# A fused attention and FFN kernel: FFN blocks of 384 tokens with 128-wide f tiles, operands placed at multiples of 512 bytes, and x split at the turn of blocks

## The chip, the cores and the metric

The kernel runs on one core of one Trainium2 chip. The metric is the device time of one execution in microseconds (us). Three executions of the kernel before took 975.67, 976.66 and 978.05 us, a median of 976.66 us.

## What is computed

The inputs q, k and v have 8 batches, 8 heads, 576 positions and a head size of 64. The output of the attention, reshaped to 4608 tokens of 512 values, is the x of a feed-forward layer (FFN) with 2048 hidden values.

```python
q_d, k_d, v_d = mean of q, k, v over groups of 4 positions        # 144 positions
out_up = np.repeat(softmax_attention(q_d, k_d, v_d), 4, axis=2)
mask = np.abs(pos[:, None] - pos[None, :]) < 4                    # 7 neighbours
out_local = softmax(where(mask, 0.125 * q @ k.T, -1e9)) @ v
x = (out_up + out_local).transpose(0, 2, 1, 3).reshape(4608, 512)
h = x @ w_in                                                      # 512 -> 2048
g = s * maximum(h, 0) ** 2 + b
out = g @ w_out                                                   # 2048 -> 512
```

## The kernel before

**The FFN.** Every float32 operand of the FFN is split into a high part in the type float32r and a low part, and each product is made of three matmuls (high by high, high by low, low by high). The tokens go in 18 blocks of 256 (`TB`), and the 2048 hidden values in 8 tiles of 256, numbered p. One step is one block t and one tile p. `gemm1(t, p)` makes 24 matmuls of 256 columns (lines 544 to 546): two halves j of the f tile, four k tiles, three products each. The stationary operand is a 128x128 piece of `wi`, the moving one is 256 tokens of `xh` or `xl`. ScalarE then makes relu, square and the high part `gh` (lines 554 to 556), VectorE the low part `gl` (line 557); every third of these pairs from block 3 on is one tile `gb` instead. `gemm2(t, p)` (lines 589 to 591) makes 12 matmuls of 512 columns: two groups m of 128 tokens, two halves j, three products. Here `gh` or `gl` is stationary and `wo` is moving, and the sum stays in PSUM over all eight p, one bank for each m. In all there are 3456 matmuls of 256 columns and 1728 of 512. After the last p VectorE scales the sums and adds the bias into `os` (lines 596 and 601), and SyncE's queue stores it.

**The split of x.** `split_x(t)` makes `xh` on ScalarE (line 530, one copy of 128x1024, two where a block crosses a batch) and `xl` on VectorE (line 531). From block 3 on it is called three steps before the block begins (`splits`), into tiles with two buffers, so a block's x stands ready while the one before it is still multiplied.

**The attention.** The 12 pairs of heads of the first three batches are done by `first_unit`, whose local part runs on TensorE; the other 20 pairs, two at a time, by `two_pairs`, whose local part runs on GpSimd (`pr`, line 455; part of `acc`, line 477) and VectorE (`st`, line 457; `pv`, line 476), seven neighbours at a time. `advance` hands out pieces of the attention between the steps of the FFN so that a batch is complete a few steps before its tokens are needed (`need`, `free`).

**The order.** The instructions of each engine are put in order at build time from the order in the code and priorities (`tc.high_priority`), and run in that order, each waiting on semaphores. For steps from block 3 on, `gemm2` follows its `gemm1` by three steps (`pend`).

**Where the tiles lie.** Pools hand out SBUF addresses at build time. Start addresses modulo 512 bytes in each partition, read from the two built programs:

| tile | before | after |
|---|---|---|
| wi, wo of p = 2 to 6 | 352 | 0 |
| wi, wo of p = 0, 1, 7 | 480 | 0 |
| xh, xl, gh, gl | 288 | 0 |
| xh, xl of block 2; gb; os | 352 | 0 |

Every 128-column slice of these tiles is 512 bytes long, so the slices that a matmul reads have the remainder of their tile. Before, all these remainders are 32 modulo 64.

Of the kernel before, what the change touches and what calls it, by code (L numbers as in the profile page):

```python
# [10 lines left out]
F32 = mybir.dt.float32  # L11
# [24 lines left out]
TB = 256  # L36
NB = NT // TB
# [14 lines left out]
BEHIND = {1: 400, 2: 100, 4: 100, 5: 400}  # L52
HF = 7
# [4 lines left out]
OB = {0: (0, 1), 1: (2, 3), 2: (6, 7)}  # L58
# [3 lines left out]
def attention_ffn_kernel(ctx, tc, qk, vw_in, vr_in, vdm, qkn, vn, w_in, w_out, s_in, b_in, out):  # L62
# [24 lines left out]

    def make_room(i):
        sc, dg = flat(f"wi{6 - i}", 2048), flat(f"wo{6 - i}", 2048)
# [41 lines left out]
    mask = cst.tile([P, 3, 32], F32, name="mask")  # L131
# [103 lines left out]
    def split_w(p):  # L235
        with tc.high_priority(offset=-BEHIND.get(p, 0)):
            split_parts(p)
# [95 lines left out]
    def first_unit(b, hp, banks):  # L333
# [75 lines left out]
        ups = tmp([P, SD], "ups")  # L409
# [107 lines left out]
    def split_x(t):  # L517
        tags = ("os", "xl2") if t == 2 else ("xh", "xl")
        pool = one if t == 2 else two
        xh = pool.tile([P, HP, TB], F32R, tag=tags[0], name="xh")  # L520
        xl = pool.tile([P, HP, TB], F32R, tag=tags[1], name="xl")
        t0 = t * TB
        while t0 < (t + 1) * TB:
            b = t0 // S
            while (b, HP - 1) not in complete:
                next(gen)
            n = min((t + 1) * TB, (b + 1) * S) - t0
            src = xt[b][:, :, t0 - b * S : t0 - b * S + n]
            dst = slice(t0 - t * TB, t0 - t * TB + n)
            nc.scalar.copy(xh[:, :, dst], src)  # L530
            nc.vector.tensor_tensor(
                xl[:, :, dst], src, xh[:, :, dst].bitcast(F32), ALU.subtract)
            t0 += n
        xs[t] = (xh, xl)
# [4 lines left out]
    def gemm1(t, p):  # L539
        xh, xl = xs[t]  # L540
        ph = bank(6 if t >= 3 and p % 2 else 7 if t == 1 and p < HF else 4, [P, 2, TB], "ph")
        for j, k in itertools.product(range(2), range(NK)):
            f = slice(P * j, P * j + P)
            nc.tensor.matmul(ph[:, j], wi[p][:, 0, k, f], xh[:, k], start=(k == 0), stop=False)  # L544
            nc.tensor.matmul(ph[:, j], wi[p][:, 0, k, f], xl[:, k], start=False, stop=False)  # L545
            nc.tensor.matmul(ph[:, j], wi[p][:, 1, k, f], xh[:, k], start=False, stop=(k == NK - 1))  # L546
        if t >= 3 and p % 3 == 2:
            both = one.tile([P, 2, 2, TB], F32R, tag="xl2", name="gb")
            gh, gl = both[:, 0], both[:, 1]
        else:  # L550
            gh = two.tile([P, 2, TB], F32R, tag="gh", name="gh")
            gl = two.tile([P, 2, TB], F32R, tag="gl", name="gl")
# [5 lines left out]
        gt[(t, p)] = (gh, gl)  # L558
# [15 lines left out]
    def gemm2(t, p):  # L574
        if (t, p) == (0, NFP - 1):
            column_sums()
        gh, gl = gt.pop((t, p))
        if p == 0:
            ob = OB.get(t, OB[0])
            oacc[t] = [bank(i, [P, DM], "po") for i in ob]  # L580
        po = oacc[t]
        end = t == NB - 1 and p == NFP - 1
        os_ = one.tile([P, 2, DM], F32, tag="os", name="os") if p == NFP - 1 else None
        for m in range(2):
            ms = slice(P * m, P * m + P)
            for j in range(2):
                first = p == 0 and j == 0
                last = p == NFP - 1 and j == 1
                nc.tensor.matmul(po[m], gh[:, j, ms], wo[p][:, 0, j], start=first, stop=False)  # L589
# [9 lines left out]
        if p == NFP - 1 and not end:  # L599
            for m in range(2):  # L600
                nc.vector.scalar_tensor_tensor(
                    os_[:, m], po[m], sb_s, bias, ALU.mult, ALU.add)
# [155 lines left out]
```

## Time and profile before

| | |
|---|---|
| median of three runs | 976.66 us |
| the profiled execution's own time | 974.94 us |
| its span, first to last instruction | 973.1 us |
| mean granted TensorE clock | 0.982 |
| busy: TensorE | 937.4 us (96%) |
| busy: VectorE | 646.8 us (66%) |
| busy: ScalarE | 478.8 us (49%) |
| busy: GpSimd | 425.0 us (44%) |

The profile is one execution, recorded instruction by instruction. In its rows PE is the matmuls of TensorE, PEld its weight loads, DVE is VectorE, ACT ScalarE, POOL GpSimd and SP SyncE; an engine with a q behind it is its queue. `out<-in` are the names of tiles, and a shape is partitions by elements. A row of the timeline gives the start in us, the duration in us, and the instruction; rows that follow on the same line are merged, with their number behind the x. The recorded end of a matmul is modelled and overlaps its successors (a matmul of 256 columns is given 0.28 us, while the next one starts 0.11 to 0.12 us later). So the distance from start to start, not the duration, tells how fast matmuls flow.

### The profile page before, as it was taken

The page shows a single profiled execution, that of the slowest core. Times are in us where ns is not written, and L with a number is a line of the kernel's source. Part 1 is how long each engine was busy: PE and PEld are TensorE (multiplying, and loading weights), DVE is VectorE, ACT ScalarE, POOL GpSimd, SP SyncE. Part 2 cuts the span into 40 slices and gives each one's busy share as a digit, 9 for nine tenths or more (in the row PEclk, how much of TensorE's full clock was granted, in tenths as well). Part 3 has the DMA queues.
Part 4 walks back from the last instruction along what each step waited for, and adds up shares of the span by engine and source line. Part 5 has one row for each costly group of instructions (what it writes and reads, how often), then busy time and mean ns, then how long its engine had stood idle before and what let it go on. Part 6 is the DMA issues. An engine that isn't in the chain of part 4 may idle for free.

```text
span 973.1 us, 18535 instructions
## 1 busy us (share of the span) xinstructions
PE 937.4 (96%) x7316; PEld 840.0 (86%) x7316; DVE 646.8 (66%) x1175; ACT 478.8 (49%) x1141; POOL 425.0 (44%) x455
## 2 busy tenths in 40 slices
PE   5769999999999999999999999999999999999998
PEld 4558888788999989889989898999899999998997
DVE  5999985864468778878787975876787772211121
ACT  5878775453755454534545344454454444333231
POOL 9422011100167686776767585575776750000000
PEclk9579999999999999999999999999999999999999
DMA  9746422102233232322323232231323100000000
GB/s 314 261 132 204 166 65 73 60 31 86 88 122 112 86 101 85 133 65 72 106 93 102 80 98 80 78 112 58 112 90 111 55 23 1 23 1 22 1 23 22
DMA packets 32103, 86.26 MB, mean 89 GB/s; under 512 B 3344, under 2 KB 7952, under 8 KB 32016
## 3 DMA queue, kind: packets, MB, share of 16 engines
q1 hardware_dynamic: 32016, 85.08, 26.4%
q8 instruction: 57, 0.93, 0.4%
q14 instruction: 30, 0.25, 0.1%
HBM read 75.63 MB, written 9.44 MB: 87 GB/s over the span
## 4 chain that ended last, share of the span: by engine, by line
PE 76%; DVE 7%; POOL 6%; DMA 6%; issue 3%; ACT 2%; DVEq 0%; SPq 0%; POOLq 0%; ACTq 0%
PE ph L544 12%; PE ph L545 12%; PE ph L546 12%; PE po L589 11%; PE po L590 11%; PE po L591 11%; DMA tqk<-in_qk_dram 3%; POOL pr L455 2%; PE sa L297 2%; DMA lqk<-in_qkn_dram 1%; POOL acc L477 1%; DMA wst<-in_moe_w_out_dram 1%; PE up L328 1%; PE ol L420 1%; PE ot L486 1%
## 5 line engine op out<-in xcount | busy, mean ns | idle before, releaser
L544 PE MATMUL ph<-xh,wi 128*128 128x256 f32 x1152 | 327.2, 284 | 5.3 <-DVE gl L557 2.5
L545 PE MATMUL ph<-xl,wi 128*128 128x256 f32 x1152 | 324.0, 281 | 0.0
L546 PE MATMUL ph<-xh,wi 128*128 128x256 f32 x1152 | 323.6, 281 | 0.0
L455 POOL TENSOR_TENSOR pr<-lqk 128x576 f32<-128x576 f32 x140 | 203.0, 1473 | 90.1 <-DMA lqk<-in_qkn_dram 53.9
L544 PEld LDWEIGHTS ph<-xh,wi 128*128 128x128 f32 x1152 | 217.1, 188 | 12.8 <-DVE gl L557 3.4
L545 PEld LDWEIGHTS ph<-xl,wi 128*128 128x128 f32 x1152 | 217.0, 188 | 5.0 <-issue 0.2
L546 PEld LDWEIGHTS ph<-xh,wi 128*128 128x128 f32 x1152 | 217.3, 189 | 0.1
L554 ACT ACTIVATE ph<-ph 128x512 f32<-128x512 f32 x144 | 83.7, 581 | 236.7 <-PE ph L546 236.5
L589 PE MATMUL po<-wo,gh 128*128 128x512 f32 x456 | 183.0, 402 | 0.2 <-ACT gh L556 0.2
L590 PE MATMUL po<-wo,gh 128*128 128x512 f32 x456 | 181.5, 398 | 0.0
L591 PE MATMUL po<-wo,gl 128*128 128x512 f32 x456 | 179.5, 399 | 0.0
L557 DVE TENSOR_TENSOR gl<-ph,gh 128x512 fp32r<-128x512 f32 x114 | 77.9, 683 | 110.9 <-ACT gh L556 110.5
L477 POOL TENSOR_TENSOR acc<-acc,pv 128x576 f32<-128x576 f32 x80 | 114.6, 1433 | 68.0 <-DVE acc L477 33.5
L457 DVE TENSOR_REDUCE st<-pr 128x9 f32<-128x576 f32 x140 | 105.9, 756 | 40.9 <-POOL pr L455 38.8
L287 POOL TENSOR_TENSOR dq<-vq 64x64 f32<-64x64 f32 x58 | 25.6, 441 | 192.4 <-PE up L326 190.2
L556 ACT CAST gh<-ph 128x512 fp32r<-128x512 f32 x114 | 66.8, 586 | 70.6 <-PE po L590 68.5
L591 PEld LDWEIGHTS po<-wo,gl 128*128 128x128 f32 x456 | 85.7, 188 | 17.3 <-issue 0.2
L476 DVE TENSOR_TENSOR pv<-lv,st 128x576 f32<-128x576 f32 x120 | 87.2, 747 | 20.2 <-POOL acc L477 19.6
L589 PEld LDWEIGHTS po<-wo,gh 128*128 128x128 f32 x456 | 85.7, 188 | 15.8 <-ACT gh L556 0.8
L590 PEld LDWEIGHTS po<-wo,gh 128*128 128x128 f32 x456 | 85.8, 188 | 15.6
L555 ACT ACTIVATE ph<-ph 128x512 f32<-128x512 f32 x144 | 83.8, 582 | 3.4
L590 PE MATMUL po<-wo,gb 128*128 128x512 f32 x120 | 48.2, 402 | 0.0
(145 smaller groups left out, 1261.1 us busy)
## 6 DMA issues: line engine op xcount, KB each, us to landing
tqk<-in_qk_dram SPq DMA_DIRECT2D x30, 584.0 KB, 4.0
lqk<-in_qkn_dram SPq DMA_DIRECT2D x20, 768.0 KB, 4.4
lv<-in_vn_dram SPq DMA_DIRECT2D x20, 480.0 KB, 3.5
out_dram<-os SPq DMA_DIRECT2D x17, 512.0 KB, 3.0
wst<-in_moe_w_in_dram SPq DMA_DIRECT2D x7, 1024.0 KB, 5.5
wst<-in_moe_w_out_dram SPq DMA_DIRECT2D x7, 1024.0 KB, 5.3
tvd<-in_vdm_dram SPq DMA_DIRECT2D x29, 160.0 KB, 2.7
tvr<-in_vr_dram SPq DMA_DIRECT2D x29, 128.0 KB, 2.1
```

The source lines that it names most:

```text
L455: nc.gpsimd.tensor_tensor(pr, lqk[:, 0:CH], lqk[:, CH + o : 2 * CH + o], ALU.mult)
L457: nc.vector.tensor_reduce(ls[:, :, o], pr, AX.X, ALU.add)
L476: nc.vector.tensor_tensor(pv, lv[:, o : o + CH], w, ALU.mult)
L477: (nc.vector if o % 3 == 1 else nc.gpsimd).tensor_tensor(acc[:, :, h], acc[:, :, h], pv, ALU.add)
L544: nc.tensor.matmul(ph[:, j], wi[p][:, 0, k, f], xh[:, k], start=(k == 0), stop=False)
L545: nc.tensor.matmul(ph[:, j], wi[p][:, 0, k, f], xl[:, k], start=False, stop=False)
L546: nc.tensor.matmul(ph[:, j], wi[p][:, 1, k, f], xh[:, k], start=False, stop=(k == NK - 1))
L554: nc.scalar.activation(ph, ph, AF.Relu)
L555: nc.scalar.activation(ph, ph, AF.Square)
L589: nc.tensor.matmul(po[m], gh[:, j, ms], wo[p][:, 0, j], start=first, stop=False)
L590: nc.tensor.matmul(po[m], gh[:, j, ms], wo[p][:, 1, j], start=False, stop=False)
L591: nc.tensor.matmul(po[m], gl[:, j, ms], wo[p][:, 0, j], start=False, stop=last)
```

## The change

The first three blocks keep 256 tokens and their steps. From token 768 on there are ten blocks of 384 tokens, 13 blocks in all. A step of these has one 128-wide f tile: `gemm1` makes 12 matmuls of 384 columns, `gemm2` 9 of 512 (three groups m of 128 tokens). There are 16 such steps to a block, 160 in all. Blocks of 384 keep three PSUM banks (0, 1, 2) for the sums, and the attention of the later batches cycles through two banks (3, 5) where it had three. Small unused tiles (`skip`) of 32, 448 and 96 bytes move the FFN's tiles to the remainders in the table above; to make room, the attention's `mask` shares the place of `pv`, and `ups` that of `ptm`. From block 3 on x is split in two halves of two k tiles each, with two buffers for a half, so a half can be written only when the block before has finished with that half: `split_x(n + 1)` is called at the last step of block n (the turn), at high priority, and there two `gemm2` are taken from `pend` instead of one. Each group m of `os` is stored by its own DMA, and the third group uses the place of the first.

```diff
-TB = 256
-NB = NT // TB
+BLOCKS = [(t, 256) for t in range(0, 768, 256)] + [(t, 384) for t in range(768, NT, 384)]
+NB = len(BLOCKS)
...
+AHEAD = 6
+SKIP = (32, 448, 96)
-OB = {0: (0, 1), 1: (2, 3), 2: (6, 7)}
+OB = {0: (0, 1), 1: (2, 3), 2: (6, 7), 3: (0, 1, 2)}
...
+    def skip(n, pool=one):
+        pool.tile([P, n // 4], F32, tag=f"skip{n}", name="skip")
...
-    def split_x(t):
-        tags = ("os", "xl2") if t == 2 else ("xh", "xl")
...
+    def split_x(n):
+        t0, nt = BLOCKS[n]
+        nk = NK if n < 3 else NK // 2
+        hs, ls = [], []
+        for k0 in range(0, NK, nk):
+            tags = ("os", "xl2") if n == 2 else ("xh", "xl")
+            pool = one if n == 2 else two
+            xh = pool.tile([P, nk, nt], F32R, tag=tags[0], name="xh")
+            xl = pool.tile([P, nk, nt], F32R, tag=tags[1], name="xl")
...
+                src = xt[b][:, k0 : k0 + nk, at - b * S : at - b * S + m]
+                nc.scalar.copy(xh[:, :, dst], src)
+                nc.vector.tensor_tensor(
+                    xl[:, :, dst], src, xh[:, :, dst].bitcast(F32), ALU.subtract)
...
+    def tiles(n, i):
+        return (i, (0, 1)) if n < 3 else (i // 2, (i % 2,))
+
+    def gemm1(n, i, st):
+        p, js = tiles(n, i)
+        shape = [P, len(js), BLOCKS[n][1]]
...
-        for m in range(2):
+        for m in range(nt // P):
...
+                nc.vector.scalar_tensor_tensor(
+                    os_[:, m % 2, cs], po[m][:, cs], sb_s, bias[:, cs], ALU.mult, ALU.add)
+                nc.sync.dma_start(out[r0 : r0 + P, cs], os_[:, m % 2, cs])
...
-    need = [0, 2 * HF - 3] + [(S * b // TB) * NFP - 3 for b in range(2, B)]
-    free = [0, 0, 16] + [((S * (b - 1) - 1) // TB) * NFP - 2 for b in range(3, B)]
-    rings = {1: banks(5, 6), 2: banks(5), 3: banks(2, 3, 5)}
+    need = [0, 2 * HF - 3] + [begin(S * b) - (10 if b == 2 else AHEAD) for b in range(2, B)]
+    free = [0, 0, 16] + [max(need[b - 1], begin(S * (b - 1) - 1) - AHEAD) for b in range(3, B)]
+    rings = {1: banks(5, 6), 2: banks(5), 3: banks(3, 5)}
...
-    splits = {(1, HF - 1): 2, (2, NFP - 2): 3}
-    splits.update({(t, NFP - 3): t + 1 for t in range(3, NB - 1)})
+    splits = {(1, HF - 1): 2}
...
+        turn = 2 <= n < NB - 1 and i == (NFP if n < 3 else 2 * NFP) - 1
+        if turn:
+            with tc.high_priority():
+                split_x(n + 1)
-        if len(pend) > (2 if t < 3 else 3):
+        while len(pend) > (2 if n < 3 or turn else 3):
             gemm2(*pend.pop(0))
```

The changed file is longer, so its line numbers are higher: lines 544 to 546 of `gemm1` become 571 to 573, lines 554 to 557 become 581 to 584, lines 589 to 591 of `gemm2` become 618 to 620, lines 530 and 531 of `split_x` become 549 and 550, and line 601 becomes 629.

How the order changes is shown at three places. First TensorE, where the last block begins; the numbers behind names tell one buffer's use from another's. Before, the first matmul of the block (`ph_10502`) follows the second product group of a `gemm2`:

```order
L589 MATMUL po_10314<-wo_1446,gh_10352 128x512
L590 MATMUL po_10314<-wo_1446,gh_10352 128x512
L591 MATMUL po_10314<-wo_1446,gl_10353 128x512
L544 MATMUL ph_10502<-xh_10412,wi_705 128x256 [waits DVE_49]
L545 MATMUL ph_10502<-xl_10413,wi_705 128x256
L546 MATMUL ph_10502<-xh_10412,wi_705 128x256
```

And now, with the two halves of x in `xh_9721`, `xl_9722` and `xh_9725`, `xl_9726`:

```order
L619 MATMUL po_9388<-wo_1994,gh_9688 128x512
L571 MATMUL ph_9747<-xh_9721,wi_707 128x384 [waits DVE_49,PE_49]
L572 MATMUL ph_9747<-xl_9722,wi_707 128x384
...
L571 MATMUL ph_9747<-xh_9725,wi_707 128x384 [waits Activation_49]
L620 MATMUL po_9386<-wo_1994,gl_9689 128x512
L620 MATMUL po_9387<-wo_1994,gl_9689 128x512
L620 MATMUL po_9388<-wo_1994,gl_9689 128x512
L618 MATMUL po_9386<-wo_1994,gb_9716 128x512 [waits Activation_49]
L619 MATMUL po_9386<-wo_1994,gb_9716 128x512
L572 MATMUL ph_9747<-xl_9726,wi_707 128x384 [waits DVE_49]
```

The block's first step is now cut in three by waits on ScalarE and VectorE, with five matmuls of earlier `gemm2` between; the 18 matmuls of `gemm2` ahead of it are not all shown.

Second VectorE, where x is split while GpSimd and VectorE work on the attention. Before, one subtract of 1024 columns stands between the sums of the attention (`st`):

```order
L457 TENSOR_REDUCE st_6585<-pr_6605 128x9 [waits DVE_49]
L531 TENSOR_TENSOR xl_6891<-x_4704,xh_6890 128x1024 [waits PE_49,Activation_49]
L457 TENSOR_REDUCE st_6585<-pr_6608 128x9 [waits DVE_49,Pool_49]
L557 TENSOR_TENSOR gl_6457<-ph_6431,gh_6456 128x512 [waits PE_49,Activation_49]
L457 TENSOR_REDUCE st_6585<-pr_6655 128x9 [waits DVE_49,Pool_49]
```

And now, at the turn that begins the block of `xh_6187`:

```order
L487 TENSOR_TENSOR acc_5865<-lv_6078,st_5866 128x9x64 [waits DMAHW3_49,DVE_49]
L490 TENSOR_TENSOR pv_6213<-lv_6078,st_5866 128x576
L490 TENSOR_TENSOR pv_6216<-lv_6078,st_5866 128x576
L550 TENSOR_TENSOR xl_6188<-x_4490,xh_6187 128x768 [waits Activation_49]
L320 RECIPROCAL dsm_6109<-dsm_6109 96x3 [waits Activation_49]
L491 TENSOR_TENSOR acc_5865<-acc_5865,pv_6213 128x9x64 [waits DVE_49]
L285 TENSOR_REDUCE qd_6528<-tqk_6325 128x144 [waits DMAHW7_49]
L550 TENSOR_TENSOR xl_6192<-x_4490,xh_6191 128x768 [waits PE_49,Activation_49]
L584 TENSOR_TENSOR gl_6159<-ph_6145,gh_6158 128x384 [waits PE_49,Activation_49]
```

The two halves stand behind work of the attention, one of them behind an instruction that waits for a DMA.

Third VectorE again, where a block's sums leave PSUM near the end. Before, both groups leave one behind the other:

```order
L557 TENSOR_TENSOR gl_10176<-ph_10150,gh_10175 128x512 [waits DVE_49,PE_49,Activation_49]
L601 SCALAR_TENSOR_TENSOR os_10266<-po_9961,sb_s_168,bias_143 128x512 [waits DMAHW2_49,PE_49]
L601 SCALAR_TENSOR_TENSOR os_10266<-po_9962,sb_s_168,bias_143 128x512 [waits PE_49]
L557 TENSOR_TENSOR gl_10219<-ph_10193,gh_10218 128x512 [waits DVE_49,Activation_49]
L557 TENSOR_TENSOR gb_10261<-ph_10236,gb_10261 128x512 [waits PE_49,Activation_49]
```

And now:

```order
L584 TENSOR_TENSOR gl_9761<-ph_9747,gh_9760 128x384 [waits DVE_49,PE_49,Activation_49]
L629 SCALAR_TENSOR_TENSOR os_9812<-po_9386,sb_s_169,bias_144 128x512 [waits DMAHW1_49,DMAHW0_49,PE_49]
L629 SCALAR_TENSOR_TENSOR os_9812<-po_9387,sb_s_169,bias_144 128x512 [waits PE_49]
L584 TENSOR_TENSOR gl_9780<-ph_9766,gh_9779 128x384 [waits DVE_49,Activation_49]
L629 SCALAR_TENSOR_TENSOR os_9812<-po_9388,sb_s_169,bias_144 128x512 [waits DMAHW2_49,DVE_49,PE_49]
```

The third group's instruction has a wait for a DMA, the store of the first group.

More of the change, by code (lines that the diff above doesn't have):

```diff
@@ L536, in attention_ffn_kernel @@
     gt = {}
     oacc = {}
[L539 to L548, printed above, removed]
+    def tiles(n, i):
+        return (i, (0, 1)) if n < 3 else (i // 2, (i % 2,))
@@ new lines, in gemm1 @@
+    def gemm1(n, i, st):
+        xh, xl = xs[n]
+        p, js = tiles(n, i)
+        shape = [P, len(js), BLOCKS[n][1]]
+        ph = bank(6 if n >= 3 and i % 2 else 7 if n == 1 and p < HF else 4, shape, "ph")
+        for j, k in itertools.product(js, range(NK)):
+            o, f = ph[:, js.index(j)], slice(P * j, P * j + P)
+            nc.tensor.matmul(o, wi[p][:, 0, k, f], xh[k], start=(k == 0), stop=False)
+            nc.tensor.matmul(o, wi[p][:, 0, k, f], xl[k], start=False, stop=False)
+            nc.tensor.matmul(o, wi[p][:, 1, k, f], xh[k], start=False, stop=(k == NK - 1))
+        if n >= 3 and st % 3 == 2:
+            both = one.tile([P, 2, *shape[1:]], F32R, tag="xl2", name="gb")
@@ L572, in column_sums, with gemm2 @@
         nc.vector.tensor_scalar(bias, cs, sb_b, None, ALU.mult)
-    def gemm2(t, p):
-        if (t, p) == (0, NFP - 1):
+    def gemm2(n, i):
+        if (n, i) == (0, NFP - 1):
             column_sums()
[L577 to L583, printed above, removed]
-        for m in range(2):
-            ms = slice(P * m, P * m + P)
[L586 to L589, printed above, removed]
-                nc.tensor.matmul(po[m], gh[:, j, ms], wo[p][:, 1, j], start=False, stop=False)
-                nc.tensor.matmul(po[m], gl[:, j, ms], wo[p][:, 0, j], start=False, stop=last)
-            if end:
-                r0 = TB * t + P * m
-                for c in (0, DM // 2):
-                    cs = slice(c, c + DM // 2)
-                    nc.vector.scalar_tensor_tensor(
-                        os_[:, m, cs], po[m][:, cs], sb_s, bias[:, cs], ALU.mult, ALU.add)
-                    nc.sync.dma_start(out[r0 : r0 + P, cs], os_[:, m, cs])
-        if p == NFP - 1 and not end:
-            for m in range(2):
@@ new lines, in gemm2 @@
+        gh, gl = gt.pop((n, i))
+        p, js = tiles(n, i)
+        t0, nt = BLOCKS[n]
+        if i == 0:
+            oacc[n] = [bank(j, [P, DM], "po") for j in OB[min(n, 3)]]
+        po = oacc[n]
+        done = p == NFP - 1 and js[-1] == 1
+        end = done and n == NB - 1
+        if done:
+            os_ = one.tile([P, 2, DM], F32, tag="os", name="os")
+        for m in range(nt // P):
+            ms = slice(P * m, P * m + P)
+            for c, j in enumerate(js):
+                first, last = i == 0 and c == 0, done and j == 1
+                nc.tensor.matmul(po[m], gh[:, c, ms], wo[p][:, 0, j], start=first, stop=False)
+                nc.tensor.matmul(po[m], gh[:, c, ms], wo[p][:, 1, j], start=False, stop=False)
+                nc.tensor.matmul(po[m], gl[:, c, ms], wo[p][:, 0, j], start=False, stop=last)
+            if not done:
+                continue
+            if end and m == 2:
+                os_ = one.tile([P, 2, DM], F32, tag="big", name="os")
+            r0 = t0 + P * m
+            w = DM // 2 if end and m == 2 else DM
+            for c in range(0, DM, w):
+                cs = slice(c, c + w)
```

59 lines of the change are left out of this document (29 added, 30 removed).

## The prediction

> **What bounds the kernel now.** I read the busy table and the slices first:
>
> ```profile
> PE 937.4 (96%) x7316; PEld 840.0 (86%) x7316; DVE 646.8 (66%) x1175; ACT 478.8 (49%) x1141; POOL 425.0 (44%) x455
> ...
> PEclk9579999999999999999999999999999999999999
> ```
>
> TensorE is busy almost throughout and its clock is full after the first slices. The windows by stage say the same:
>
> ```profile
> 40.00:100.00 60.00, 47.61 (x525) 42.06 (x526) 59.19 (x119) 47.96 (x105) 13.09 (x14) 0.83 0.50 168
> 100.00:300.00 200.00, 197.87 (x1898) 173.74 (x1898) 140.11 (x269) 115.50 (x280) 39.45 (x54) 1.00 0.24 80
> 300.00:760.00 460.00, 457.23 (x3051) 414.88 (x3050) 356.03 (x618) 216.25 (x534) 316.29 (x293) 1.00 0.29 93
> 760.00:969.00 209.00, 209.00 (x1352) 188.99 (x1351) 62.43 (x108) 73.38 (x144) 25.78 (x23) 1.00 0.05 17
> ```
>
> From 100 us on TensorE is idle for about 1% of a window or less. VectorE, in third place, is busy 77% of the stretch from 300 to 760 us, GpSimd, in fifth, 69%. The waits of TensorE hold almost nothing that belongs to the FFN:
>
> ```profile
> PE ph L544 <- DVE gl L557: 2.5, 3, 1.2
> ```
>
> So the time is set by how fast the FFN's matmuls follow each other, and that is read from start to start. TensorE's rows late in the program, where the attention is over, at places that I name below:
>
> ```profile
> 938.76 0.28 PE L544 MATMUL ph<-xh,wi 128*128 128x256 f32 x1
> ...
> 939.46 0.28 PE L544 MATMUL ph<-xh,wi 128*128 128x256 f32 x1
> ...
> 941.50 0.39 PE L589 MATMUL po<-wo,gh 128*128 128x512 f32 x1
> ...
> 948.42 0.39 PE L589 MATMUL po<-wo,gb 128*128 128x512 f32 x1
> ...
> 949.78 0.28 PE L544 MATMUL ph<-xh,wi 128*128 128x256 f32 x1
> ...
> 952.61 0.40 PE L589 MATMUL po<-wo,gh 128*128 128x512 f32 x1
> ```
>
> A step of `gemm1`, 24 matmuls, takes 2.74 us from 938.76 to 941.50 (0.1142 each; its last 18, from 939.46, 0.1133) and 2.83 us from 949.78 to 952.61 (0.1179), though nothing is waited for and the shapes are the same. Six of `gemm2` take 1.36 us from 948.42 to 949.78 (0.2267 each). The last 48 matmuls of the program are all of `gemm2`:
>
> ```profile
> 958.21 0.39 PE L589 MATMUL po<-wo,gh 128*128 128x512 f32 x1
> ...
> 966.45 0.40 PE L589 MATMUL po<-wo,gh 128*128 128x512 f32 x1
> ...
> 967.85 0.40 PE L589 MATMUL po<-wo,gh 128*128 128x512 f32 x1
> ```
>
> ```profile
> 969.02 0.39 PE L591 MATMUL po<-wo,gl 128*128 128x512 f32 x1
> ```
>
> From the first to the last, 47 distances, it is 10.81 us, 0.2300 each, and the six from 966.45 take 0.2333 each. Block 2, whose x lies elsewhere, gives a third pace for 256 columns:
>
> ```profile
> 200.67 0.28 PE L545 MATMUL ph<-xl,wi 128*128 128x256 f32 x1
> ...
> 203.43 0.39 PE L591 MATMUL po<-wo,gl 128*128 128x512 f32 x1
> ```
>
> That is 23 distances in 2.76 us, 0.1200 each. With 0.116 for 256 columns (between the two late steps) and 0.230 for 512, the FFN takes 3456 x 0.116 + 1728 x 0.230 = 798 us of the span of 973.1.
>
> **The change part by part. The pace.** The same shapes go at 0.1133, 0.1179 and 0.1200, and at 0.2267 and 0.2333. The extremes lie 6.7 and 6.6 ns apart, so the loss seems to come in pieces of 6.7 ns. What differs between these steps is where the operands lie and how the matmuls came in from the step before. If the best rows hold one such piece in 256 columns and two in 512, then 0.1067 and 0.2133 are left without loss, both 0.417 ns a column. That is an estimate, but another row supports it. The attention's plain float32 transposes run slowly enough per column not to be pressed:
>
> ```profile
> 377.40 1.20 PE L486 MATMUL ot<-ident,acc 128*128 128x128 f32 x9
> 378.35 0.36 PE L544 MATMUL ph<-xh,wi 128*128 128x256 f32 x1
> ```
>
> Nine of 128 columns take 0.95 us, 0.825 ns a column. Half of that is 0.4125, if float32r goes at twice the pace of plain float32. No row shows float32r matmuls with operands at multiples of 512 bytes, so the ends are these. Low: 0.4125 ns a column, 0.1056, 0.1584 and 0.2112 for 256, 384 and 512. High: 0.1200, its 1.5 times 0.1800, and 0.2333. After the change there are 24 steps with 24 matmuls of 256 (576), 160 steps with 12 of 384 (1920), and still 1728 of 512. The low end is 60.8 + 304.1 + 364.9 = 730 us, a gain of 68; the high end is 69.1 + 345.6 + 403.1 = 818, a loss of 20. I take 0.422 ns a column, 0.108, 0.162 and 0.216, which is nearer to the transposes' row than to the best float32r row (0.443): the loss changes with placement, and now every slice begins on a 512-byte line and ends on one. That makes 62.2 + 311.0 + 373.2 = 746 us, **a gain of 52**. Fewer and longer matmuls are in this count; by columns alone `gemm1` has as many as before.
>
> The page TensorE: Matmul & The Clock Gate of the Trainium skill, section Back-to-back issue gap, gives N/2.4 + 2.5 ns as the isolated gap from matmul to matmul on the warm clock. By it the FFN would take 62.9 + 312.0 + 372.9 = 748 us; the rows above lie 4 to 10% over it, and it says nothing of addresses.
>
> **The turn.** Ten times x is now split with TensorE at the end of a block, where it was done three steps ahead. Each half costs a copy on ScalarE and a subtract on VectorE:
>
> ```profile
> L531 DVE TENSOR_TENSOR xl<-x,xh 128x1024 fp32r<-128x1024 f32 x12 | 26.3, 2188 | 12.5 <-ACT xh L530 12.4
> ...
> L531 DVE TENSOR_TENSOR xl<-x,xh 128x512 fp32r<-128x512 f32 x4 | 2.7, 686 | 1.8 <-ACT xh L530 1.8
> ...
> L530 ACT CAST xh<-x 128x768 fp32r<-128x768 f32 x4 | 3.3, 829 | 1.0 <-DVE x L423 0.6 <-DVE x L490 0.4
> ```
>
> The first half is free after six of the last step's twelve matmuls. A copy of 0.83 and a subtract of about 1.03 (1.5 times 0.686) make it ready 1.9 us later; the second half is free 1.0 us later and, behind a relu, ready 3.3 us after the first was freed. TensorE has six matmuls of `gemm1` and 18 of `gemm2` to do first, 0.97 + 3.89 = 4.9 us. Without other work on VectorE the turn costs nothing. But while GpSimd works the subtract is stretched:
>
> ```profile
> 532.55 5.79 DVE L531 TENSOR_TENSOR xl<-x,xh 128x1024 fp32r<-128x1024 f32 x1
> ```
>
> The mean of 1024 columns above is 2.19 us, this one took 5.79. At that rate a half takes 4.3 us, and instructions of the attention stand ahead of it. Token 4032, the first of the last batch, lies in block 11, so the attention ends six steps before that block, and eight of the ten turns have it beside them. At worst each is late by about 4 us, at best by nothing: 0 to 32 us. I take 1 us each, **a cost of 8**, nearer the low end since TensorE also has five matmuls of `gemm2` to put between.
>
> **The shorter step and the stores.** A step falls from 24 x 0.116 + 12 x 0.230 = 5.5 us to 12 x 0.162 + 9 x 0.216 = 3.9. A bank of `ph` is used again two steps later, so relu, square, copy and `gl` must be through in about 5.8 us where they had 8.3.
>
> ```profile
> L554 ACT ACTIVATE ph<-ph 128x512 f32<-128x512 f32 x144 | 83.7, 581 | 236.7 <-PE ph L546 236.5
> ...
> L557 DVE TENSOR_TENSOR gl<-ph,gh 128x512 fp32r<-128x512 f32 x114 | 77.9, 683 | 110.9 <-ACT gh L556 110.5
> ...
> L556 ACT CAST gh<-ph 128x512 fp32r<-128x512 f32 x114 | 66.8, 586 | 70.6 <-PE po L590 68.5 <-PE po L591 1.0
> ...
> L601 DVE SCALAR_TENSOR_TENSOR os<-po,sb_s,bias 128x512 f32<-128x512 f32 x34 | 24.8, 743 | 7.0 <-PE po L591 4.6 <-DMA out_dram<-os 2.4
> ```
>
> The relu, a square like it, the copy and `gl` take 0.58 + 0.58 + 0.59 + 0.68 = 2.4 us at 512 columns and less at 384, so they fit unless VectorE's queue holds several us of attention. The same attention in a stretch that is 6% shorter makes VectorE 82% and GpSimd 74% busy there. The third group of a block's sums waits for the store of the first:
>
> ```profile
> out_dram<-os SPq DMA_DIRECT2D x17, 512.0 KB, 3.0
> ```
>
> A store lands 3.0 us after its issue, and the third sum is done 1.3 us after the first, so VectorE can stand for some 2 us nine times; queued behind it are `gl` of the next steps, and TensorE waits for these only after its 5.8 us are gone. I put this at nothing; with that cover gone it would be 18. For the whole paragraph I take **a cost of 6**, between 0 and 20. The two-bank ring of the attention and the moved tiles `mask` and `ups` I put at nothing: the matmuls that they could delay stand between FFN matmuls that hide them.
>
> **The sum** for the profiled execution is 974.9 - 52 + 8 + 6 = 937 us. The median of the runs lies 1.7 above that execution, so I predict **939 us**, with a range of its own from 920 to 955 (a gain of 68 and a cost of 12, a gain of 45 and a cost of 24).
>
> **The rivals.** (1) Only the best pace of today is reached everywhere: 0.1133, 0.170 and 0.2267. Then the FFN is 65.3 + 326.4 + 391.7 = 783, a gain of 15 against a cost of 14: 976 us. For it speaks that all rows of float32r lie at or over 0.443 ns a column, against it that the loss comes in pieces that change with the steps. (2) The pace is reached, but from 300 to 760 us the attention on VectorE and GpSimd and the turns take its place as the bound. About half the gain is lost, 26 us, and the turns cost their 14: 974.9 - 26 + 14 + 1.7, some 965 us. For it speaks VectorE's 77%, against it that TensorE hardly waits for it now. (3) Slower: moving and stationary operands now have the same remainder. Block 2 with p 2 to 6 is the one place where x and `wi` have that today (352 and 352), and it has the slowest pace, 0.1200. If `gemm1` goes so everywhere, with 0.1800 for 384 columns, and `gemm2` at 0.2267 (where `gb` and `wo` have the same remainder), the FFN is 69.1 + 345.6 + 391.7 = 806, and with 14 of costs the time is 999 us. It decides from 0.1704 us for 384 columns upward. Against it speaks that the 0.2267 with equal remainders is the best pace of 512. (4) Placement has no part in it, and a column costs what it costs today: 798 us again, with the costs 991 us. The different paces of equal shapes speak against it.
>
> The page SBUF — State Buffer of the Trainium skill, section Who interferes with whom, is on the side of (4): TensorE has separate read ports for the moving and the stationary operand and waits for no one. The trace does not bear that out as far as equal shapes at full clock go at 0.1133 and 0.1200.
>
> **How the numbers follow.** The forecast has a chance of 0.54, rival (1) 0.13, (2) 0.15, (3) 0.12, (4) 0.06. A measurement of this kernel can tell about 0.2%, 2 us, from no change. Faster by more are the forecast, (2) and 0.06 of (1), together 0.75; (1) lies within 0.2% with 0.04; slower are 0.03 of (1), (3) and (4), 0.21. The range from 918 to 983 takes in the forecast, (1) and (2), and leaves out (3) and (4) and a little at the low end.
>
> **What would show it.** In the profile after, 12 matmuls of `gemm1` should span 1.94 us and 9 of `gemm2` 1.94 us, in the first three blocks 24 should span 2.6. If they span over 2.04 and 2.04, the pace has failed and with it the forecast. At the turns TensorE's idle time in front of line 572 should add up to under 12 us, and most of it before the attention ends; waits of line 571 for `gl` should stay under some 6 us. If the pace is right and the time is over 955, the idle time of TensorE names rival (2).

## The result: 986.54 us, 1.15% slower

The changed kernel takes 986.54 us (median of 4 runs, 985.53 to 986.8), the kernel before it 976.16 in the same session: a ratio of 1.0115, with a 95% interval from 1.0098 to 1.0133. The profiled execution took 985.53 us with a span of 983.7, so 10.6 us more than the one before.

The page after, its row of TensorE and the granted clock in 40 slices:

```profile
PE 942.8 (96%) x6356; PEld 842.6 (86%) x6356; DVE 649.7 (66%) x1220; ACT 493.8 (50%) x1267; POOL 422.1 (43%) x455
...
PEclk9969999999999999899999999999999999999999
```

TensorE has 960 matmuls fewer and is busy as long as before. In slice 17, at about 400 us, the clock has a dent that it hadn't. The windows by stage (the last one is a stretch of that slice) and TensorE's waits with the FFN and the end of a batch:

```profile
100.00:300.00 200.00, 198.23 (x1819) 173.30 (x1816) 129.44 (x253) 112.78 (x278) 28.79 (x46) 1.00 0.23 74
300.00:760.00 460.00, 452.25 (x2412) 408.76 (x2411) 352.86 (x641) 220.05 (x599) 309.88 (x287) 0.99 0.28 93
760.00:979.00 219.00, 218.85 (x1129) 198.14 (x1127) 78.62 (x146) 87.86 (x207) 41.55 (x36) 1.00 0.07 24
398.60:405.40 6.80, 5.29 (x16) 4.41 (x17) 6.38 (x14) 4.27 (x16) 3.39 (x3) 0.50 0.39 125
```

```profile
PE ph L571 <- ACT xh L549: 3.9, 2, 2.7
...
PE tp L329 <- ACT pd L322: 2.7, 2, 1.4
...
PE ph L571 <- DVE gl L584: 2.0, 2, 1.1
PE ot L500 <- DVE x L504: 1.8, 1, 1.8
```

The longer of the two waits for `xh`, 2.7 us, lies at 64 us, where the kernel before has one of 2.3; the turns have only the other, 1.26 us.

Behind 760 us TensorE still has nothing to wait for, and the pace can be read there. The first rows of two steps of the first gemm, and of the 18 matmuls of the second that follow them:

```profile
902.97 0.33 PE L571 MATMUL ph<-xh,wi 128*128 128x384 f32 x1
...
905.05 0.86 PE L620 MATMUL po<-wo,gb 128*128 128x512 f32 x3
...
909.17 0.33 PE L571 MATMUL ph<-xh,wi 128*128 128x384 f32 x1
```

Twelve matmuls of 384 columns take 2.08 us, 173.3 ns each, where 162 were forecast; 18 of 512 take 4.12, 229 ns each, where 216 were forecast. In the first blocks the 256-column matmuls settle at 120.0 ns. Worked out from every start-to-start distance inside a gemm behind 760 us, the means are 116.6 ns (798 distances) and 231.7 (410) before, and 176.3 (537) and 230.9 (422) after. The same work, 24 and 12 matmuls for 256 tokens, takes 24 x 116.6 + 12 x 231.7 = 5.58 us before and 4/3 x (12 x 176.3 + 9 x 230.9) = 5.59 us after. **The pace gave nothing at all.**

The 10.6 us come from elsewhere. Most of them lie at the turn into the block of token 1536, which is the first to hold tokens of batch 3:

```profile
394.50 0.40 PE L620 MATMUL po<-wo,gl 128*128 128x512 f32 x1
395.12 1.09 PE L500 MATMUL ot<-ident,acc 128*128 128x128 f32 x8 [0.22 <-POOL acc L491]
398.03 0.30 PE L500 MATMUL ot<-ident,acc 128*128 128x128 f32 x1 [1.82 <-DVE x L504]
398.69 1.72 PE L311 MATMUL sa<-kd,dq 128*96 128x144 f32 x6 [0.36 <-DVE x L504]
401.67 1.01 PE L571 MATMUL ph<-xh,wi 128*128 128x384 f32 x2 [1.26 <-ACT xh L549]
402.84 0.69 PE L572 MATMUL ph<-xl,wi 128*128 128x384 f32 x1 [0.16 <-DVE xl L550]
...
405.25 0.41 PE L571 MATMUL ph<-xh,wi 128*128 128x384 f32 x1
```

The attention of batch 3 ends here (line 500), x is split only then, and TensorE has nothing else left to do. From 398.6 us the clock is at half for 6.8 us, in which matmuls of 384 columns are 320 ns apart. From 394.50 to 405.25, 10.75 us, it does one matmul of the second gemm, nine transposes (0.95 us in the row of 377.40 before), six `sa` and nine of `gemm1`, some 3.4 us of work: 7.4 us are lost. Smaller stretches are at 700 to 704 us (waits for `pd` and `gl`, 2.9 us) and at the end:

```profile
978.01 0.84 PE L620 MATMUL po<-wo,gl 128*128 128x512 f32 x3
```

```profile
978.43 2.19 DVE L629 SCALAR_TENSOR_TENSOR os<-po,sb_s,bias 128x512 f32<-128x512 f32 x4 [2.27 <-PE po L620]
```

All four last sums wait for the last three matmuls and follow each other on VectorE. From the last matmul's start to the end of the span it is 5.3 us (978.46 to 983.75), where it was 4.1. The three places make 11.5 us; the rest of the program is 0.9 faster.

### The profile page after: what moved, and what is told of

Its sections match the earlier page's. It is cut to its first block, busy times and chain, and to the rows that moved or that the text cites. A ratio compares the mean times of both kernels' runs of the same rounds, so it can differ in the third digit from the quotient of the medians.

```text
span 983.7 us, 16869 instructions
## 1 busy us (share of the span) xinstructions
PE 942.8 (96%) x6356; PEld 842.6 (86%) x6356; DVE 649.7 (66%) x1220; ACT 493.8 (50%) x1267; POOL 422.1 (43%) x455
## 4 chain that ended last, share of the span: by engine, by line
PE 76%; DVE 9%; DMA 5%; POOL 5%; ACT 3%; issue 2%; SPq 0%; DVEq 0%; ACTq 0%; POOLq 0%
PE ph L571 12%; PE ph L572 12%; PE ph L573 12%; PE po L618 11%; PE po L619 11%; PE po L620 11%; POOL pr L469 2%; DMA tqk<-in_qk_dram 2%; PE sa L311 2%; DMA flat<-in_vr_dram 1%; POOL acc L491 1%; PE up L342 1%; PE ol L434 1%; PE ot L500 1%; DVE pv L490 1%
## 5 line engine op out<-in xcount | busy, mean ns | idle before, releaser
L571 PE MATMUL ph<-xh,wi 128*128 128x384 f32 (+1 forms) x832 | 275.2, 331 | 6.0 <-ACT xh L549 3.9
L572 PE MATMUL ph<-xl,wi 128*128 128x384 f32 (+1 forms) x832 | 271.9, 327 | 0.2 <-DVE xl L550 0.2
L573 PE MATMUL ph<-xh,wi 128*128 128x384 f32 (+1 forms) x832 | 271.5, 326 | 0.0
L581 ACT ACTIVATE ph<-ph 128x384 f32<-128x384 f32 (+1 forms) x184 | 89.8, 488 | 293.1 <-PE ph L573 279.6
L571 PEld LDWEIGHTS ph<-xh,wi 128*128 128x128 f32 x832 | 157.8, 190 | 13.9 <-ACT xh L549 4.6
L618 PE MATMUL po<-wo,gh 128*128 128x512 f32 x417 | 166.6, 400 | 0.3 <-ACT gh L583 0.2
L619 PE MATMUL po<-wo,gh 128*128 128x512 f32 x417 | 164.4, 394 | 0.0
L572 PEld LDWEIGHTS ph<-xl,wi 128*128 128x128 f32 x832 | 157.7, 190 | 6.6 <-DVE xl L550 0.7
L573 PEld LDWEIGHTS ph<-xh,wi 128*128 128x128 f32 x832 | 157.6, 189 | 0.7
L620 PE MATMUL po<-wo,gl 128*128 128x512 f32 x417 | 156.8, 395 | 0.0
L491 POOL TENSOR_TENSOR acc<-acc,pv 128x576 f32<-128x576 f32 x80 | 116.5, 1456 | 93.4 <-DVE acc L491 56.5
L584 DVE TENSOR_TENSOR gl<-ph,gh 128x384 fp32r<-128x384 f32 (+1 forms) x131 | 75.5, 577 | 109.8 <-ACT gh L583 109.0
L582 ACT ACTIVATE ph<-ph 128x384 f32<-128x384 f32 (+1 forms) x184 | 90.1, 490 | 4.5
L583 ACT CAST gh<-ph 128x384 fp32r<-128x384 f32 (+1 forms) x131 | 65.1, 498 | 14.9 <-PE po L619 11.0
L584 DVE TENSOR_TENSOR gb<-ph,gb 128x384 fp32r<-128x384 f32 x53 | 29.3, 552 | 53.5 <-ACT gb L583 53.2
```

The source lines that it names most:

```text
L491: (nc.vector if o % 3 == 1 else nc.gpsimd).tensor_tensor(acc[:, :, h], acc[:, :, h], pv, ALU.add)
L571: nc.tensor.matmul(o, wi[p][:, 0, k, f], xh[k], start=(k == 0), stop=False)
L572: nc.tensor.matmul(o, wi[p][:, 0, k, f], xl[k], start=False, stop=False)
L573: nc.tensor.matmul(o, wi[p][:, 1, k, f], xh[k], start=False, stop=(k == NK - 1))
L582: nc.scalar.activation(ph, ph, AF.Square)
L584: nc.vector.tensor_tensor(gl, ph, gh.bitcast(F32), ALU.subtract)
```

## The experiments

Two questions: why didn't longer blocks and multiples of 512 bytes raise the pace, and what made the turn dear? Times are medians, ratios are to the kernel before on the same chip (974.6 us with the first four kernels, 975.6 with the next, 975.0 with the rest).

**m1_pace**, bare matmuls, 24 of each setting:

```
+ s0 = base // 4 + 128 * (i % 8); m0 = (base + d) // 4 + 512 * (i % 2)
+ nc.tensor.matmul(po[:, 0:w], st[:, s0 : s0 + 128], mv[:, m0 : m0 + w], ...)
```

> This kernel leaves out the whole computation: it loads a little data and then runs 24 float32r matmuls per setting without waits, with 256, 384 or 512 columns, the stationary operand starting at 0 or 32 bytes past a multiple of 512, and the moving operand a set difference (0 to 480 bytes) from it. Read is the spacing of matmuls per setting. Theory A (the loss per matmul hangs on the difference of the two operands' remainders and not on the columns; in the trace after the change it is 120.0, 173.3 and 226.7 ns for 256, 384 and 512 columns at difference 0): at difference 0 those three numbers for both starts; at some other differences up to 13 ns less for every width, that is 107, 160 and 213 ns at the best. Theory C (starting at a multiple of 512 is what counts): the start at 0 is faster than the start at 32 at the same difference, by several ns, and the loss grows with the columns. Theory B (placement plays no part): the same spacing within 1 ns for all 24 settings of a width.

TensorE's rows. A name holds the columns, the stationary operand's start past a multiple of 512 bytes and the difference of the moving one; the second number is the time of the 24:

```profile
31.75 3.00 PE L47 MATMUL n256b0d192x<-mv,st 128*128 128x256 f32 x24
34.81 3.13 PE L47 MATMUL n256b0d256x<-mv,st 128*128 128x256 f32 x24
...
69.57 3.00 PE L47 MATMUL n256b32d192x<-mv,st 128*128 128x256 f32 x24
72.63 3.13 PE L47 MATMUL n256b32d256x<-mv,st 128*128 128x256 f32 x24
...
88.36 4.43 PE L47 MATMUL n384b0d0x<-mv,st 128*128 128x384 f32 x24
```

```profile
106.44 4.50 PE L47 MATMUL n384b0d96x<-mv,st 128*128 128x384 f32 x24
...
196.88 5.73 PE L47 MATMUL n512b0d0x<-mv,st 128*128 128x512 f32 x24
...
232.15 5.87 PE L47 MATMUL n512b0d192x<-mv,st 128*128 128x512 f32 x24
...
337.98 2.93 PE L54 MATMUL n256m32d0x<-mv,st 128*32 128x256 f32 x24
...
349.93 4.35 PE L54 MATMUL n384m32d0x<-mv,st 128*32 128x384 f32 x24
```

The start past 512 bytes makes no difference (rows b0 and b32 are alike); the difference between the operands does. In the single starts a setting settles after a few matmuls: 256 columns at 113.3 ns with a difference of 192 or 448 and at 120.0 with 0 or 256; 384 columns at 173.3 with 0, 64, 256, 320 or 480 and at up to 177 on average with others; 512 at 226.7 with 0 or 256 and at 229 to 234 with the rest. From 173.3 to 226.7 it is 53.3 ns for 128 columns, 0.4167 a column, so 106.7, 160 and 213.3 would be without loss. The loss is then 6.7 to 13.3 ns with 256 columns and **never under 13.3 with 384 or 512**. Theory A is right that the difference counts and the start doesn't, and wrong that other differences save up to 13 ns at every width. C and B fall. A stationary operand of 32 columns (the names with m32), with a quarter of the weights' columns to load, settles at the same 173.3 with 384 columns, but at 113.3 instead of 120.0 with 256 and at 231.5 instead of 226.7 with 512, all at difference 0. So the loss depends on the loaded weights too, in no direction that holds for all widths.

**m2_fine**, the same with five widths and steps of 16 bytes.

> Like the first kernel of spacings this one leaves out the whole computation; now for 256, 320, 384, 448 and 512 columns and all differences of the operands' remainders from 0 to 240 in steps of 16. Theory F (a float32r matmul costs its columns plus a fixed 13.3 ns at best, and only narrow ones get below that): 113.3 ns for 256 at a difference of 192 and about 120 elsewhere, 173.3 at the best for 384, 226.7 at the best for 512, and for 320 and 448 columns 146.7 and 200.0 at difference 0 with nothing over 2 ns below that. Theory G (each width has a difference of its own at which half of the loss goes, which steps of 64 missed): 384 columns reach 166.7 and 512 columns 220.0 at some step of 16.

Of 16 differences each, the mean of the last 15 distances is 113.3 to 119.9 ns for 256 columns, 145.3 to 153.3 for 320, 173.3 to 179.9 for 384, 200.0 to 206.7 for 448, and 226.7 to 234.3 for 512. Against 0.4167 ns a column the loss is at least 6.7, 12, 13.3, 13.3 and 13.3 ns. Theory F holds and G falls; only F's details are off: with 448 columns difference 0 is among the slowest (206.7) and 64 and 160 give the 200.0, and with 256 columns 112 and 32 lie at 114.5 and 116.5 instead of about 120.

**e1_old_rem**, the changed kernel with the old remainders:

```
- SKIP = (32, 448, 96)
+ SKIP = (384, 64, 0)
```

> The kernel after the change, with the operands put back to the remainders they had before it (288, 352 and 480) and the same order of instructions. Theory A (equal remainders of moving and stationary operand cost up to 13 ns a matmul, whatever the columns): most of the 256-column matmuls go from 120.0 to about 117 ns and most of the 384-column ones from 173.3 to about 170, some 4400 matmuls by about 2 to 3 ns, so 974 to 979 us. Theory B (placement plays no part): 986.5 us. Theory C (multiples of 512 gain something that another part of the change has eaten): slower than 986.5, about 995 us or more.

988.83 us, 1.0146 [1.0122, 1.0169]. Theory A falls as a theory of the changed kernel: the 384-column matmuls stay at a mean of 176.3 ns behind 760 us, as in the changed kernel, since they have no better setting than the one it gave them. The turn at 395 us lies here too, with half clock for 10.2 us where the changed kernel has 6.8, and a second stretch of half clock at 705, which can make the run slower still:

```profile
705.60:712.20 6.60, 5.95 (x17) 5.56 (x18) 5.30 (x10) 2.37 (x7) 5.54 (x4) 0.50 0.32 120
398.40:408.40 10.00, 7.90 (x26) 6.28 (x27) 8.25 (x21) 5.93 (x20) 5.33 (x5) 0.50 0.45 165
```

**e2_before_512**, the kernel before with the changed kernel's placement alone:

```
- mask = cst.tile([P, 3, 32], F32, name="mask")
+ mask = two.tile([P, 3, 32], F32, tag="pv", name="mask")
...
+ skip(SKIP[2], two)
```

> The kernel before the change with its order of instructions kept and all matmul operands of the FFN put at multiples of 512 bytes. Theory A: the 256-column matmuls of the first gemm go from a mean of 116.7 to 120.0 ns (some 3100 of them, about +10 us) and the 512-column ones from 232.3 to about 228 (some 800 to 1600 of them, about -3 to -6 us), so 979 to 985 us. Theory B: 976 us. Theory C: a gain, 930 to 965 us.

980.37 us, 1.0059 [1.0039, 1.0078], inside theory A's numbers and against C's. Equal remainders everywhere make the 256-column matmuls slower (120.1 ns on the mean behind 760 us, 116.6 before) and the 512-column ones a little faster (230.0 against 231.7).

**e4_before_x192**, the same with x's operands moved by 64 bytes:

```
- SKIP = (32, 448, 96)
+ SKIP = (32, 448, 64, 32)
...
+ skip(SKIP[3], two)
```

> The kernel before the change with its order of instructions; wi, wo, gh, gl and gb begin at multiples of 512 bytes as in the second run, and x's split operands 192 bytes off a multiple of 256. Theory P (the spacing that the bare matmuls show carries over): 3264 matmuls of the first gemm go from 120.0 to 113.3 ns, 22 us off the 980.4 of the second run, so 957 to 960 us, which is below both kernels. The rival (in the kernel the other order of weights and the traffic of the other engines set the pace): 972 to 980 us.

969.47 us, 0.9934 [0.9914, 0.9955]: faster than both kernels, but half of what theory P promised. Starts of a step of this kernel, and of the second run's:

```profile
880.44 0.28 PE L554 MATMUL ph<-xh,wi 128*128 128x256 f32 x1
...
883.27 0.39 PE L599 MATMUL po<-wo,gh 128*128 128x512 f32 x1
...
885.31 0.28 PE L554 MATMUL ph<-xh,wi 128*128 128x256 f32 x1
```

```profile
882.89 0.28 PE L554 MATMUL ph<-xh,wi 128*128 128x256 f32 x1
...
885.76 0.40 PE L599 MATMUL po<-wo,gh 128*128 128x512 f32 x1
```

The 24 take 2.83 us, 117.8 each, not the 113.3 of the bare stream, against 2.87 in the second run. The nine of the second gemm take 2.04, 226.7 each. The kernel before goes at 113.3 in some steps and at 117.8 in others (the prediction's rows). In its last three blocks the steps at 113.3 to 114.2 on the mean are those with p 2 to 5, x at 288 and `wi` at 352: a difference of 448, the very one that gives 117.8 here. And p 6, with the same two starts, goes at 117.7 there. So the same offsets hold more than one steady pace; that the matmuls ahead of a step decide which is the reading that the next run puts to the test.

**m3_steps**, steps of both gemms in the kernel's shapes without waits (the scheduler wove steps of both widths together, so a step's predecessor is not always its like):

```
+ for dg in G256:
+     for dx in X256:
+         for _ in range(2):
+             step(256, dx, dg, (0, 1))
```

> This kernel leaves out the attention, the activations and all checks of values: it runs only steps of the FFN's matmuls in the kernel's order (24 of 256 columns and 12 of 512, then 12 of 384 and 9 of 512) without waits, with x and gh moved in steps of 16 bytes against wi and wo. Theory L (each matmul's loss follows from the operands' remainders and from the phase in which the stream comes in from the matmul before, so the same remainders hold more than one steady pace): x 192 bytes off with gh at 0 gives 117.8 ns as in the kernel, not the 113.3 of the bare stream, and another pair of offsets gives 113.3 and 226.7 together, 5.44 us for a step of 24 and 12 (5.55 at 117.8). Theory F (the remainders alone decide): 192 gives 113.3 here. For 384 columns both expect nothing below 173.3.

In the second of the two steps of a setting, x 192 off with gh at 0 gives 117.8 and 226.7 ns, as in the kernel, and all at 0 gives 119.7 and 228.9, as in the second run (119.7 and 227.8 in its late steps). With gh 16 off the same x gives 113.6 (117.9 in the first of the two steps), and 232.2 for the second gemm. So far theory L. No setting gives 113.3 and 226.7 together: of 64 settings a step of 24 and 12 takes 5.50 us at the best (x 112, gh 16) and 5.68 at the worst. A step of 12 of 384 and 9 takes 4.13 to 4.21. For the same work, 4/3 of it, that is 5.51 to 5.61: **the wide blocks have no better setting than the narrow ones.** The changed kernel's own, all at 0, is 4.17 (5.56).

**e10_before_x112**:

```
+ both = two.tile([P, 2 * HP * TB + 16], F32R, tag="xx", name="xx")
+ o = 12 if (t - (t > 2)) % 2 == 0 else 4
```

> The kernel before the change with its order of instructions, wi, wo, gh, gl and gb at multiples of 512 bytes, and x's two split operands as the parts of one tile, 112 bytes off a multiple of 256 in one buffer and 144 in the other. Theory L (remainders and the phase of entry together set the pace, as the steps without waits show it): a step of 24 and 12 goes from 5.55 us with x 192 off to 5.51 and 5.52, 5 us over 144 steps, so 963 to 967 us. The rival (in the whole kernel other work breaks up what the bare steps show): 969 to 976 us.

972.57 us, 0.9969 [0.9955, 0.9983]. Theory L's size is missed. In the undisturbed stretch the pace is there:

```profile
824.18 0.28 PE L561 MATMUL ph<-xx,wi 128*128 128x256 f32 x1
...
826.94 0.39 PE L606 MATMUL po<-wo,gb 128*128 128x512 f32 x1
...
829.69 0.28 PE L561 MATMUL ph<-xx,wi 128*128 128x256 f32 x1
```

2.76 + 2.75 = 5.51 us, as the bare steps have it. But from 300 to 760 us, with the attention's matmuls between, the means are 118.8 and 232.2 ns, and 118.7 and 231.8 in the run with x 192 off: no gain. Why it is 3 us slower than that run is open.

**e11_after_x64**, the changed kernel with x 64 off:

```
- skip(SKIP[2], two)
  split_x(0)
  split_x(1)
+ skip(SKIP[2], two)
```

> The kernel after the change with the same order of instructions and x's split operands 64 bytes off a multiple of 256, all others at multiples of 512. Theory L: a step of 12 and 9 goes from 4.17 to 4.13 us and one of 24 and 12 from 5.62 to 5.59, 160 x 0.04 + 24 x 0.03 = 7 us, so 978 to 981 us, with the waits at 395 us as they were. The rival: 984 to 988 us.

983.93 us, 1.0085 [1.0067, 1.0103], some 3 us under the changed kernel (1.0115) instead of 7. Behind 760 us the means fall by 1.7 and 2.0 ns, from 300 to 760 by 0.1 and 1.2. Its profile has a second stretch of half clock, 3.4 us at 703 us, which takes some of that back. It is slower than before all the same.

Now the turn. **e3_no_resplit**:

```
+ if turn and n > 2:
+     xs[n + 1] = xs[3]
- if turn:
+ elif turn:
```

> The kernel after the change, without the splits of x at the turns behind the fourth block: later blocks read the fourth block's split operands, so these splits are left out and later blocks compute on old data. Theory T (the 10 us that the change lost come from the turns, above all the one at 395 to 406 us with the half clock that follows it): the waits at 323 and 395 us go, 978 to 980 us. The rival (the turns' waits are replaced by others as soon as they go, since attention is late there anyway and the PE waits on its softmax): 984 to 987 us.

972.77 us, 0.9989 [0.9978, 1.0001]. More goes than theory T said: 1.26% against the changed kernel, 12 us. Behind 300 us no two matmuls are over 0.5 us apart, and the clock stays full from 71 to 969 us. **e9_no_split5** leaves out one of these splits:

```
+ if turn and n == 4:
+     xs[5] = xs[4]
- if turn:
+ elif turn:
```

> The kernel after the change without the split of x at one turn, the one into the block at token 1536 (that block computes on the operands of the block before, all else is there). Theory T (that turn's waits and the half clock behind them make most of the loss): 977 to 980 us. The rival (the eight other turns cost as much together): 983 to 986 us, and the run without any later split, at 972.8, stays 10 us below it.

980.33 us, 1.0062 [1.0047, 1.0077], between the two theories' numbers: that turn costs 0.53%, 5 us, and the others with their work 7. Where these 7 lie is not shown in full. In this run's profile TensorE waits 1.1 us for `xl` in front of line 572 and 0.7 for `gb`, where the changed kernel has 0.2 and none, so later turns cost something of their own.

**e5_ahead10** and **e6_ahead14** let each batch's attention end earlier in the program:

```
- AHEAD = 6
+ AHEAD = 10
```

> The kernel after the change with each batch's attention ending ten steps ahead of its block instead of six. Theory T (the attention of a batch ends too late for the turn into its block, TensorE stands and its clock falls to half): the waits and the half clock at 395 us go, 976 to 981 us. The rival (VectorE and GpSimd have no room from 300 to 760 us, so earlier work only moves the waits): 984 to 989 us.

> As the run before, with fourteen steps. Theory T: no more than that run gains, 976 to 981 us. The rival: 984 to 992 us, since the attention of the early batches is pushed into the first blocks.

985.84 us (1.0097 [1.007, 1.0125]) and 985.73 (1.0098 [1.0079, 1.0118]): theory T's remedy does nothing. The rows of the attention's final transposes, from 320 to 405 us, in the changed kernel and with ten steps:

```profile
L500 PE MATMUL ot<-ident,acc x18: 270/272/329, 345.8 to 398.0; 128*128 128x128 f32 x18
```

```profile
L500 PE MATMUL ot<-ident,acc x18: 270/272/301, 345.5 to 397.7; 128*128 128x128 f32 x18
```

The two units of batch 3 end at the same times, 50 us apart, wherever the program puts them. In the kernel before they end sooner:

```profile
L486 PE MATMUL ot<-ident,acc x18: 271/273/328, 327.9 to 378.3; 128*128 128x128 f32 x18
```

The change took a PSUM bank from the attention's ring for the third accumulator. **e8_before_ring2** does that alone, **e7_ot_third** gives the changed kernel's transposes a third bank:

```
- rings = {1: banks(5, 6), 2: banks(5), 3: banks(2, 3, 5)}
+ rings = {1: banks(5, 6), 2: banks(5), 3: banks(3, 5)}
```

```
- ot = banks([P, n, P], "ot")
+ ot = bank(7, [P, n, P], "ot") if i0 == 0 else banks([P, n, P], "ot")
```

> The kernel before the change with the attention's ring cut from three PSUM banks to two, as the change does. Theory R: 3 to 8 us slower than before, 979 to 984 us. Rival T: within 2 us of before, 974 to 978 us.

> The kernel after the change, with the first transposes of each attention unit in a third PSUM bank (7) beside the ring of two. Theory R (the third bank that the change took from the attention's ring makes the ninth transpose wait for VectorE at 395 us): the waits there shrink by 2 to 4 us and the half clock behind them goes, 977 to 982 us. Rival T (TensorE has to wait there for the split of x whatever the banks): 984 to 988 us.

974.33 us (0.9998 [0.9987, 1.0008]) and 988.36 (1.0145 [1.0128, 1.0162], batch 3 ends at 399.8 us): theory R falls as put. But in the kernel before the ring of two does end batch 3 later, by 13 us:

```profile
L486 PE MATMUL ot<-ident,acc x18: 270/272/299, 341.2 to 391.0; 128*128 128x128 f32 x18
```

With x split three steps ahead that is just early enough. Why the smaller ring delays it, no run tells. So the ring and the turn may be harmful only together. **e12_before_turn** puts the split to the end of a block in the kernel before, **e13_before_turn_ring2** adds the ring of two:

```
- splits.update({(t, NFP - 3): t + 1 for t in range(3, NB - 1)})
...
+ if 3 <= t < NB - 1 and p == NFP - 1:
+     with tc.high_priority():
+         split_x(t + 1)
```

> The kernel before the change, with x split at the end of a block instead of three steps ahead, at high priority, from the fourth block on; three PSUM banks in the attention's ring. Theory J (the ring of two lets the attention of batch 3 end some 13 us later, and the split at the turn has no cover for that; either alone is harmless): 974 to 978 us. Theory T (the split at the turn costs by itself): 979 to 985 us.

> As the run before, with two banks in the ring. Theory J: TensorE waits 3 to 5 us at about 391 us, its clock falls to half for 7 us behind that, 979 to 985 us. Theory T: the same as the run before within 2 us, both 979 to 985.

973.93 us (0.9988 [0.9977, 1.0]) and 982.25 (1.0073 [1.0055, 1.009]). **Either alone costs nothing, both together 7.2 us, and 8.3 more than the split at the turn alone**: theory J. The second of the two on TensorE:

```profile
389.50 1.03 PE L486 MATMUL ot<-ident,acc 128*128 128x128 f32 x8
391.26 0.30 PE L486 MATMUL ot<-ident,acc 128*128 128x128 f32 x1 [0.72 <-DVE x L490]
392.58 0.95 PE L297 MATMUL sa<-kd,dq 128*96 128x144 f32 x6 [1.02 <-DVE x L490]
394.23 0.50 PE L544 MATMUL ph<-xh,wi 128*128 128x256 f32 x2 [0.70 <-ACT xh L530]
398.20 0.58 PE L545 MATMUL ph<-xl,wi 128*128 128x256 f32 x1 [3.47 <-DVE xl L531]
```

That is the changed kernel's sequence at 395 us, made from the kernel before by these two edits: the last transposes, then the split, then half clock (from 395.1 us for 6.8). One thing differs: the longest wait here, 3.47 us, is for `xl`, where the changed kernel with its split in halves waits 0.16. With three banks the same transposes end at 379.8 us, 11.5 sooner, and x is split behind them without a wait of the next block:

```profile
L486 PE MATMUL ot<-ident,acc x18: 271/272/329, 329.7 to 379.8; 128*128 128x128 f32 x18
```

No run gives the changed kernel itself a ring of three for the whole attention; for it, that both are needed is carried over from the kernel before.

## Why the prediction was wrong

**The bound** was read rightly: the FFN's matmuls set the time before and after.

**The pace** is the step that failed, with the whole forecast. "I take 0.422 ns a column, 0.108, 0.162 and 0.216 [...] now every slice begins on a 512-byte line and ends on one": measured are 0.120, 0.1733 to 0.176 and 0.227 to 0.231 us, a gain of 0 in place of 52. Two parts of the reasoning held. The price of a column without loss, 0.4167 ns, is what widths of 384 and 512 differ by, and the loss does move by up to a piece of 6.7 ns with placement and with the matmuls that came before, though most settings lie between two pieces. What had no row behind it was that a multiple of 512 bytes takes the loss away. The bare matmuls show that the distance to such a line has no part in it, and that one piece is the least that 256 columns keep and two the least that 384 and 512 keep. The kernel before, at 116.6 on the mean, kept about one and a half pieces of 6.7 on 256 columns (9.9 ns, 0.039 a column); the best of the change keeps 13.3 on 384 (0.035 a column). That 0.004 ns a column, some 1% of the first gemm, is all that wider blocks could bring, and the first three blocks at 120.0 and the 384-column matmuls' mean of 176.3 took it back.

By N/2.4 + 2.5 of the Trainium skill (TensorE: Matmul & The Clock Gate, Back-to-back issue gap) 384 and 512 columns would be 162.5 and 215.8 ns apart, an estimate. Its price of a column agrees with the 53.3 ns for 128 measured here; its constant was not met in any run with these operands, where it is 6.7 at the least.

**The turn**, put at 8 us, costs more: 12 us go with the splits behind the fourth block and their work, 5 of them with one turn. There the mechanism was another than the stretched subtract that the prediction named. The prediction put the two-bank ring of the attention at nothing, since what it could delay would "stand between FFN matmuls that hide them". By itself the ring costs the kernel before nothing (0.9998), as forecast, and so does the split at the turn (0.9988). In the kernel before, the ring ends the attention of batch 3 13 us later, and the split at the turn takes away the steps that covered this. In the changed kernel TensorE waits at line 500 (1.82 us) and in front of line 571 (1.26 us for `xh`) and goes on at half clock. In front of line 572, where the prediction looked, only 0.2 us were idle.

**The shorter step and the stores**, put at 6, cost some 1.2 us at the end of the program. Waits for `gl` are 2.0 us where 2.5 were before, as forecast (under 6). The 2.9 us at 700 us may belong here or to the turn there; no run tells. All costs together were put at 14 us; with a gain of nothing from the pace, the profiled execution lost 10.6 on balance.

**The rivals.** Rival (4), no gain from placement, gave 991 us and is nearest in its number. Its reason is wrong: placement alone moves the kernel before from 980.37 to 969.47. Rival (3), equal remainders, was right for 256 columns, whose 0.1200 from block 2 is exactly what came, and wrong for 384, where it put 0.1800 and 0.1733 was measured. Rival (2), the attention as the bound, is right at one place for 10 us, not for the stretch.

## What to carry to other kernels

A loss that is the same for each matmul has to be measured bare, at the widths and offsets that are meant, before blocks are changed to save it: one run of bare matmuls shows 173.3 ns at 384 columns, and the case is decided. Two edits that each cost nothing can share one cover: price the cover (when does its last producer end, when is it needed), not the edits one by one. The placement was worth more than the blocks: x 192 bytes off and the rest at equal remainders makes the kernel before 0.66% faster, in 0.9934 [0.9914, 0.9955] of its time.

## What was not expected of the hardware

- A float32r matmul with its weight load has a fixed loss of 6.7 to 13.3 ns at 256 columns and 13.3 to 21 at 384 and 512, which follows the difference of the operands' addresses modulo 256 bytes and the matmuls that came before; one pair of offsets has more than one steady pace (113.3 and 117.8). Loading 32 weight columns instead of 128 leaves it as it is at 384 columns (13.3), takes it from 13.3 to 6.7 at 256 and from 13.3 to 18 at 512.
- The clock falls before TensorE has stood for long. In the changed kernel waits of 0.22, 1.82 and 0.36 us, with a few short matmuls between, came ahead of the fall at 398.6 us; in the run with the ring of two alone 0.72 and 1.02 us close together left it full. Behind 300 us half clock lasts 3.4, 6.8 or 10.2 us in the records of these runs, in which matmuls take nearly twice their time (320 ns for 173.3 at 384 columns), on top of the waits.
- The Trainium skill (TensorE: Matmul & The Clock Gate, HAM oscillation) warns of gaps over about 3.4 us. These lengths of half clock agree with multiples of that; the longest single wait ahead of the fall was shorter.
